# Another order of score pairs, products with V and projection visits in the first attention block of a transformer layer

## The chip, the core and the metric

The kernel runs on one core of a Trainium2 chip. The metric is the device time of one execution in microseconds (us), as the median of several runs. The engines are named as in the profile: PE is TensorE (its weight loads are PEld), DVE is VectorE, ACT is ScalarE, POOL is GpSimd and SP is SyncE, which issues most of the transfers.

## What is computed

One pre-norm transformer layer on x of 2048 rows and 512 columns, in float32, without weights in the norms:

```python
h  = x + A(layernorm(x))       # 32 heads of 16, one shared K and V
h2 = h + B(layernorm(h))

# A: q = (x @ wq) per head, k = x @ wk, v = x @ wv
#    o = softmax(q k^T / 4) v ; o @ wo
# B: (gelu(x @ w_gate) * (x @ w_up)) @ w_down,  F = 1792
```

## The kernel before

**Blocks, lists and pairs.** The 2048 rows of queries are worked through in four blocks of 512. In a block there are eight groups of four heads, and for each group sixteen chunks of 128 keys. For each group and chunk there are two score steps. One score step ("s", `pace`, which calls `score` and `scores`, line L352) is a pair of products for two heads, of 128 keys by 512 queries each, into one tile s of two PSUM banks, and one exponential on ACT over 128 x 1024 elements (L356) into half of a tile p. There are three such tiles s in turn, so the score step n needs the exponential of step n - 3 to be done. After both steps of a chunk follows the product with V ("v", `finish(1)`, which calls `weigh`, L360) into the bank `acc`: the four heads of p, each in two passes, so that a v is eight records of the profile. When a group's sixteenth v is through, `evacuate` copies `acc` to oT (DVE, L373), stores it to DRAM (`acc_d`, SP, L374), and gets it back turned (oc, L384); then DVE inverts the sums (L389), divides and splits into o_hi and o_lo. The dense part reads these.

**The first block.** Only this block concerns us. While its scores run, the queries of the later blocks are still to be projected. This is a generator (`later_q` and `project_q`) that is advanced by a "visit" ("p"): usually six products of 128 x 512 (pq, L205) of one of the four column groups of a block, so that a column group takes two visits. At the end of the second, DVE splits the result into qh and ql, squares qh into qs, and SP stores three tiles of q_d (L234). pq and pqn share the one spare bank of PSUM. When a block's four column groups are through, the products of the norms (pqn, L243) follow. Then qn is copied (DVE, L247) and its maximum taken, GpSimd forms mm (L252 to L259), and DVE forms m (L270), which SP stores (L272). The products pqn follow in the same visit or in an "n" (`norm`), which runs them if they are due and does nothing otherwise. mm and m come with the visit after that.

**Who sets the order.** It is written out by hand: a string of moves for the head, and one that is run eight times, once for each group ("list"). PE, ACT, GpSimd, DVE and SP all work through their instructions in the order in which these moves emit them.

```python
OPENING = "ssspsspsp"
PERIOD = "ssvssvssvnssvvsssvsvssvssvvssspssvvsssvvsspsssvvsnssp"
moves = {"s": pace, "p": visit, "n": norm, "v": partial(finish, 1)}
for move in OPENING + PERIOD * (PER // KC):
    moves[move]()
```

The head has six s, so the lists begin with the steps 6, 38, 70 and so on (counted from 0). A v works on the oldest chunk that waits for it; about three wait at any time. The visits end before the eighth list does.

**What hangs on the count of s.** After each fourth s, `pace` takes one step of the finished groups' output (`take_out`: the return of oc, the inversions, the division) and one step of the splitting of later weights on GpSimd (`part_weights`: loads, L125 and L126, stores w_d at L460 and L466). With the 256th s the first block's work is drained, and its memory is handed to the dense part. With the 260th s `prime` issues nine loads for the dense part on SP: three of x (xb, L519), three of w1 (L501) and three of w2 (L509). From the 279th s on, the dense part's products (pp first, L751) are woven between the scores by other, fixed strings (`CYCLES`).

Of the kernel before, what the change touches and what calls it, by code (L numbers as in the profile page):

```python
# [31 lines left out]

OPENING = "ssspsspsp"

PERIOD = "ssvssvssvnssvvsssvsvssvssvvssspssvvsssvvsspsssvvsnssp"

RUNS = ((0, 1, 2, 3), (4, 5, 6, 7), (8, 9, 10, 11), (12, 13))

# [19 lines left out]
def kernel(  # L58
# [97 lines left out]
    def run(outer, first):  # L156
# [824 lines left out]
        with tc.manual_schedule(engines={mybir.EngineType.SP, mybir.EngineType.DVE}):  # L981
# [46 lines left out]
# [3 lines that stand above are left out]
# [401 lines left out]
```

## Time and profile before

| | |
|---|---|
| median of three runs | 1429.42 us (1429.18 to 1429.70) |
| profiled execution, its own time | 1433.01 us |
| its span in the profile | 1430.9 us |
| mean granted clock of PE | 0.997 |
| PE busy | 1396.5 us (98%) |
| ACT busy | 1031.6 us (72%) |
| DVE busy | 639.4 us (45%) |
| GpSimd busy | 219.4 us (15%) |
| exponentials (L356) | 1024 of 1.04 us |
| first block's lists, start of the first to end of the eighth | 60.3 to 308.8 us |

A row of the timeline has start, length, engine, line, operation, output and inputs, shape, and the number of merged instructions; in brackets stand the idle time before it and what ended that. A row of the windows has the stretch, its length, the busy time of PE, PEld, DVE, ACT and POOL with their counts, the granted clock, the DMA engines' share and GB/s.

### The profile page before, as it was taken

What the parts mean: (1) busy time and instruction counts of PE and PEld (TensorE: products, weight loads), DVE (VectorE), ACT (ScalarE), POOL (GpSimd) and SP (SyncE); (2) the same over time, 40 slices, a digit from 0 to 9 for tenths busy, and PEclk for the clock granted to TensorE, in tenths of its full rate; (3) what the DMA queues carried; (4) which work ended last, traced back from release to release, by engine and by line L of the source; (5) the groups of instructions that cost most, each with busy time, mean ns of one, the idle gap of its engine ahead of it and who ended that gap; (6) DMA issues with size and microseconds to landing.
All of it is one profiled execution on the core that took longest, in us unless ns stands there. A gap on an engine that the chain in (4) does not pass through costs nothing.

```text
span 1430.9 us, 25109 instructions
## 1 busy us (share of the span) xinstructions
PE 1396.5 (98%) x10384; PEld 752.4 (53%) x10384; DVE 639.4 (45%) x1043; ACT 1031.6 (72%) x1147; POOL 219.4 (15%) x305
## 2 busy tenths in 40 slices
PE   6999999999999999999999999999999999999998
PEld 5433333335455555545555555545555555556876
DVE  7413131224364444455364444545354453436665
ACT  7699999997877777877777777777777777752000
POOL 5587767710000000000000000000000000001000
PEclk9999999999999999999999999999999999999999
DMA  4467667634222332312422333311332333244352
GB/s 157 140 204 237 222 216 222 226 103 177 71 90 89 111 116 101 108 64 63 168 82 78 131 101 107 108 49 42 147 101 86 115 112 104 89 148 175 126 185 76
DMA packets 66930, 180.57 MB, mean 126 GB/s; under 512 B 9436, under 2 KB 9436, under 8 KB 66776
## 3 DMA queue, kind: packets, MB, share of 16 engines
q1 hardware_dynamic: 56976, 144.79, 30.4%
q0 software_dynamic: 9760, 34.08, 7.1%
q8 instruction: 84, 1.38, 0.4%
q14 instruction: 38, 0.31, 0.1%
q10 hardware_dynamic: 72, 0.00, 0.0%
HBM read 131.13 MB, written 47.71 MB: 125 GB/s over the span
## 4 chain that ended last, share of the span: by engine, by line
PE 89%; DVE 4%; ACT 3%; DMA 1%; issue 1%; SPq 0%; ACTq 0%; DVEq 0%
PE acc L360 31%; PE s L352 19%; PE pg L751 8%; PE pd L751 8%; PE pu L751 7%; PE pq L205 4%; ACT p L356 3%; PE pd L781 3%; PE pp L751 2%; PE pu L781 2%; PE pg L781 2%; DMA w<-w_d 1%; PE pk L1219 1%; PE pd_rest L793 1%; DVE ga L644 0%
## 5 line engine op out<-in xcount | busy, mean ns | idle before, releaser
L356 ACT ACTIVATE p<-s 128x1024 f32<-128x1024 f32 x1024 | 960.8, 1039 | 241.2 <-PE s L352 240.9
L360 PE MATMUL acc<-p,v_sb 128*32 128x512 f32 x4096 | 492.6, 601 | 0.0
L352 PE MATMUL s<-qg,kaug 50*128 50x512 f32 x1984 | 389.8, 427 | 4.1 <-ACT p L356 3.6
L352 PEld LDWEIGHTS s<-qg,kaug 50*128 50x128 f32 x1984 | 171.6, 184 | 286.8 <-issue 133.0
L360 PEld LDWEIGHTS acc<-p,v_sb 128*32 128x32 f32 x4096 | 110.1, 109 | 231.7 <-issue 217.3
L751 PE MATMUL pg<-x2h,w 64*128 64x512 f32 x672 | 177.1, 394 | 4.2 <-DVE g L625 3.1
L751 PE MATMUL pu<-x2h,w 64*128 64x512 f32 x672 | 175.6, 393 | 0.0
L135 POOL TENSOR_SCALAR rstd<-mv 128x1 f32<-128x1 f32 x16 | 3.5, 220 | 977.9 <-DVE mv L133 977.8
L751 PE MATMUL pd<-w,gh 64*128 64x512 f32 x624 | 124.1, 392 | 1.4 <-DVE h L681 1.4
L681 DVE TENSOR_TENSOR h<-h,pd 128x512 f32<-128x512 f32 x80 | 54.4, 686 | 149.4 <-PE pd L751 149.4
L751 PEld LDWEIGHTS pg<-x2h,w 64*128 64x128 f32 x672 | 95.8, 185 | 20.3 <-DVE g L625 6.5
L751 PEld LDWEIGHTS pu<-x2h,w 64*128 64x128 f32 x672 | 94.7, 185 | 11.4
L751 PE MATMUL pg<-x2l,w 64*128 64x512 f32 x336 | 100.3, 391 | 0.0
L751 PE MATMUL pu<-x2l,w 64*128 64x512 f32 x336 | 99.2, 391 | 0.0
L751 PEld LDWEIGHTS pd<-w,gh 64*128 64x128 f32 x624 | 68.4, 185 | 13.1 <-DVE h L681 2.7
L890 ACT ACTIVATE ga<-ga 128x512 f32<-128x512 f32 x14 | 8.8, 632 | 92.0 <-DVE ga L887 92.0
L389 DVE RECIPROCAL oc<-oc 128x128 f32<-128x128 f32 x64 | 56.6, 922 | 34.2 <-DMA oc<-acc_d 33.8
L751 PE MATMUL pd<-w,gl 64*128 64x512 f32 x312 | 71.8, 391 | 0.0
L625 DVE TENSOR_TENSOR g<-g,pg 128x512 f32<-128x512 f32 x42 | 28.7, 684 | 91.0 <-PE pg L751 91.0
L625 DVE TENSOR_TENSOR u<-u,pu 128x512 f32<-128x512 f32 x42 | 28.9, 687 | 78.7 <-PE pu L751 78.5
L621 DVE COPY g<-pg 128x512 f32<-128x512 f32 x42 | 29.0, 691 | 74.7 <-PE pg L751 74.7
L125 DVE CAST qh<-pq 128x512 fp32r<-128x512 f32 x11 | 7.6, 689 | 114.4 <-PE pq L205 114.4
(242 smaller groups left out, 1477.7 us busy)
## 6 DMA issues: line engine op xcount, KB each, us to landing
w<-w_d SPq DMA_DIRECT2D x112, 512.0 KB
w<-w_d SPq DMA_DIRECT2D x28, 1024.0 KB
qg<-q_d SPq DMA_DIRECT2D x62, 200.0 KB
q_d<-qh SPq DMA_DIRECT2D x32, 256.0 KB
acc_d<-oT SPq DMA_DIRECT2D x32, 256.0 KB
oc<-acc_d SPq DMA_DIRECT2D x128, 64.0 KB
w_d<-w_0b POOLq DMA_DIRECT2D x14, 512.0 KB, 3.8
w_d<-w_1b POOLq DMA_DIRECT2D x14, 512.0 KB, 5.6
```

Of the source, the lines that this page charges most:

```text
L205: nc.tensor.matmul(pq, wt[:, d, c * P : (c + 1) * P], xt[:, d, :], start=(n == 0), stop=(n == 3 * DC - 1),)
L352: nc.tensor.matmul(s[:, a, :], kaug[rows, kc * P : (kc + 1) * P], qg[rows, u, :], start=True, stop=True,)
L356: nc.scalar.activation(p[:, 2 * u : 2 * u + 2, :], s, AF.Exp, scale=SCALE)
L360: nc.tensor.matmul(acc[32 * j : 32 * j + 32, :], v_sb[:, kc, :], p[:, j, :], start=(kc == 0), stop=(kc == KC - 1), skip_group_check=True,)
L389: nc.vector.reciprocal(oc[:, 1, sl], oc[:, 1, sl])
L621: nc.vector.tensor_copy(half, bank)
L625: nc.vector.tensor_tensor(half, half, bank, op=ALU.add)
L681: nc.vector.tensor_tensor(hs[b, t], hs[b, t], bank, op=ALU.add)
L751: nc.tensor.matmul(bank, lhsT[r], rhs[r], start=(k == 0), stop=(k == n - 1), skip_group_check=True,)
L781: nc.tensor.matmul(bank, lhsT, rhs, start=(i == 0), stop=(i == len(ts) - 1))
L793: nc.tensor.matmul(bank, lhsT, rhs, start=(i == 0), stop=(i == len(ts) - 1))
L1219: nc.tensor.matmul(pks[b], wt[:, c, :], xt[:, c, :], start=(c == 0 and n == 0), stop=(c == DC - 1 and n == 2),)
```

## The change

One string is another. It has the same 32 s, 16 v and three p; it has three n instead of two.

```diff
-PERIOD = "ssvssvssvnssvvsssvsvssvssvvssspssvvsssvvsspsssvvsnssp"
+PERIOD = "psssvvssvnsspsssvvssvnssvssvssvvssspssvssvvnsssvvssvss"
```

Cut at the runs of s, the two lists read:

```
before  ss v ss v ss v n ss vv sss v s v ss v ss vv sss p ss vv sss vv ss p sss vv s n ss p
after   p sss vv ss v n ss p sss vv ss v n ss v ss v ss vv sss p ss v ss vv n sss vv ss v ss
```

In the orders that the two programs emit this moves more than the products. The first visit after the head (with mm and m of the first block) stands ahead of step 6 instead of behind step 24. The products pqn of the blocks 1, 2 and 3 stand ahead of the steps 63, 146 and 235 instead of 76, 164 and 256, and their mm and m ahead of the steps 70, 155 and 237 instead of 89, 165 and, as part of the drain, 256. After step 236 no visit has products any more: the "p" ahead of step 237 has mm and m alone, and the one ahead of step 251 only the bound's check; there five s follow one another. The last v of a group comes one s later, so `take_out` returns oc four steps later and behind the load of the next qg. For the eighth group, the last v stands behind the 260th s instead of ahead of it, and so `prime`'s nine loads stand ahead of the last store of oT and the last return of oc in SP's order. The rest of the program is the same.

## The prediction

> **What bounds the kernel now.** I read the page first, then the table of windows cut at the starts of the eight lists, then the timeline of one list on TensorE, then the waits at both ends of the block.
>
> ```profile
> PE 1396.5 (98%) x10384; PEld 752.4 (53%) x10384; DVE 639.4 (45%) x1043; ACT 1031.6 (72%) x1147; POOL 219.4 (15%) x305
> L356 ACT ACTIVATE p<-s 128x1024 f32<-128x1024 f32 x1024 | 960.8, 1039 | 241.2 <-PE s L352 240.9
> ```
>
> TensorE is busy for 98% of the span. ScalarE's exponentials are the other long engine, and over the whole kernel they wait 241 us for scores. The change touches only the first of four blocks, so that block has to be read by itself. A list starts with the score step ("s") 6, 38, 70 and so on. The columns are the window, its length, PE, PEld, DVE, ACT and POOL busy, the granted clock, the DMA share and GB/s.
>
> ```profile
> 60.34:92.67 32.33, 32.28 (x213) 11.71 (x212) 6.86 (x11) 29.48 (x32) 25.57 (x31) 0.95 0.54 177
> 92.67:123.46 30.79, 30.74 (x211) 11.57 (x210) 4.26 (x5) 29.82 (x33) 22.13 (x27) 1.00 0.76 251
> 279.25:308.76 29.51, 28.62 (x203) 9.80 (x203) 4.70 (x9) 28.75 (x32) 5.91 (x9) 1.00 0.42 133
> ```
>
> List 2 is 30.8 us long with TensorE full and ScalarE 1 us short of it. So TensorE's issue is the bound there, and ScalarE is close behind. Only the last list, which has one visit of the projections instead of three, has TensorE idle (0.9 us): there ScalarE bounds. The timeline of TensorE in list 2 gives the price of each piece:
>
> ```profile
> 92.67 0.74 PE L352 MATMUL s<-qg,kaug 50*128 50x512 f32 x4
> 93.33 1.06 PE L360 MATMUL acc<-p,v_sb 128*32 128x512 f32 x8
> ...
> 97.65 0.86 PE L352 MATMUL s<-qg,kaug 50*128 50x512 f32 x4
> 98.44 1.92 PE L360 MATMUL acc<-p,v_sb 128*32 128x512 f32 x16
> 100.29 0.97 PE L352 MATMUL s<-qg,kaug 50*128 50x512 f32 x6
> 101.19 1.06 PE L360 MATMUL acc<-p,v_sb 128*32 128x512 f32 x8
> 102.19 0.50 PE L352 MATMUL s<-qg,kaug 50*128 50x512 f32 x2
> 102.61 1.06 PE L360 MATMUL acc<-p,v_sb 128*32 128x512 f32 x8
> ...
> 108.83 0.50 PE L205 MATMUL pq<-xT_hi,wq_hi 128*128 128x512 f32 x1
> ...
> 110.42 0.72 PE L352 MATMUL s<-qg,kaug 50*128 50x512 f32 x4
> ...
> 120.68 1.29 PE L352 MATMUL s<-qg,kaug 50*128 50x512 f32 x6
> 121.90 0.50 PE L205 MATMUL pq<-xT_hi,wq_hi 128*128 128x512 f32 x1
> ```
>
> From start to start: two s 0.66 us (92.67 to 93.33), but 0.79 where they wait for a score buffer (97.65 to 98.44, the row is 0.86 long instead of 0.74); three s 0.90 (100.29 to 101.19), with such a wait 1.22 (120.68 to 121.90); a lone s 0.42; one product with V ("v") 1.00 (101.19 to 102.19); two v 1.85 (98.44 to 100.29); a visit ("p") 1.59. A list of before has eight twos, five threes, one lone s, six single v, five double v and three p. Two twos and one three of it wait. Sum: 6 x 0.66 + 2 x 0.79 + 4 x 0.90 + 1.22 + 0.42 + 6.00 + 9.25 + 4.77 = 30.8, which is what the windows show.
>
> **Lists 2 to 7.** The new list has the same six single and five double v and three p, but ten twos, four threes and no lone s: 10 x 0.66 + 4 x 0.90 + 6.00 + 9.25 + 4.77 = 30.22 without waits. Where would it wait? ScalarE's pace comes from this row:
>
> ```profile
> 314.22 13.86 ACT L356 ACTIVATE p<-s 128x1024 f32<-128x1024 f32 x15 [1.84 <-PE s L352]
> ```
>
> The last of 15 takes about 1.02, so 14 steps take 12.84: 0.917 us for one, 29.3 us for 32. "ss v" takes TensorE 1.66 us and ScalarE 1.83, so each of these loses 0.17 of the lead that the three score buffers give. Before, the stretch of "ss v" three times and then "ss" makes the first wait, and two others follow later in the list. The new list has that stretch once, and its other double v and visits are spread so that the lead is restored. I keep one wait of 0.13: 30.35, or 0.44 less for each list. Six lists give -2.6 us. The bounds are 30.22 (no wait) and 30.60 (three waits as before), so -3.5 to -1.2.
>
> **The start.** The first list, at 60.34 before, now begins with a visit, where before it had none until its 19th s. The visit carries mm and m of the first block too.
>
> ```profile
> 60.44 0.68 DVE L247 COPY qn<-pqn 32x512 f32<-32x512 f32 x1 [0.47 <-PE pqn L243]
> ```
> ```profile
> 57.76:61.18 3.42, 1.83 (x13) 0.73 (x15) 2.88 (x6) 1.46 (x3) 0.00 (x0) 1.00 0.80 242
> 61.18:64.59 3.41, 3.41 (x16) 0.70 (x12) 0.65 (x1) 2.62 (x4) 1.89 (x2) 0.50 0.53 190
> ```
>
> The visit's products need the one spare bank, which holds pqn until the copy ends at 61.12. They start there, and not at 60.34 as the list's first s did, which is 0.8 us of idle TensorE. They then fall into the 3.41 us in which the clock is granted at 0.50 (its window before had TensorE busy for 1.83 of 3.42, and will have less). So the visit takes 3.2 us and that s starts at about 64.4. One list of 30.4 later the second list starts at 94.8 instead of 92.67: +2.1 us. At the full clock it would be +0.7. The visit itself isn't lost: the last list lacks one for it.
>
> **List 8 and the clock.** All visits end earlier, and two "p" of the last list find no TensorE work. Where they stood five s follow one another. Before, the one such run lies just behind the block:
>
> ```profile
> 307.14 0.96 PE L352 MATMUL s<-qg,kaug 50*128 50x512 f32 x6
> ...
> 310.11 3.46 PE L360 MATMUL acc<-p,v_sb 128*32 128x512 f32 x16
> ```
> ```profile
> 306.94:310.35 3.41, 2.34 (x18) 1.01 (x18) 1.37 (x4) 3.27 (x4) 0.17 (x1) 1.00 0.30 96
> 310.35:313.76 3.41, 3.41 (x18) 0.70 (x12) 0.00 (x0) 2.02 (x3) 0.00 (x0) 0.50 0.00 0
> ```
>
> It takes 2.97 us (307.14 to 310.11), because ScalarE must empty the buffers. List 8 sums to two such runs (5.94), seven twos (4.62), two threes (1.80), 6.00 and 9.25 for the products with V, and an estimated 1.8 for the norm's product (as a v) and the last two s: 29.4, no less than ScalarE's 29.3, and about the 29.51 of before. So the block ends at 2.1 - 2.6 + 0 = -0.5 us.
>
> The windows show a second cost of such a run: after 3.41 us with TensorE busy for 2.34 the clock fell to 0.50 for the next 3.41, and ScalarE waited 1.84 us. I price one fall at 1.6. Before has one at the block's end. After has three places for one (two runs of five in list 8, one of four behind it), each only if a window happens to hold most of the run. With no fall the change stands at -2.1, with one at -0.5, with two at +1.1, with three at +2.7. One or two are likeliest, so I take the middle: **+0.3 us**.
> The Trainium skill ("TensorE: Matmul & The Clock Gate", Why this matters for your kernels) asks only for no idle gaps above about 3 us. The trace differs: the window above has TensorE idle for 1.07 us in all. By that rule no run of s would cost a clock, and the sum would be -2.1.
>
> **SyncE's queue.** The first loads of the dense part are issued at the 260th s. Before, the last product with V of the block and its output's store and return ran ahead of them; now that product is one s later, so nine loads stand in SyncE's queue ahead of the store of oT, and the return of oc behind it.
>
> ```profile
> 308.61 0.38 SPq L374 DMA_DIRECT2D acc_d<-oT  x1
> 315.11 1.92 SPq L384 DMA_DIRECT2D oc<-acc_d  x4
> 317.51 0.35 SPq L519 DMA_DIRECT2D xb<-in_A_x_dram  x1
> ```
> ```profile
> 323.50:334.50 11.00, 10.59 (x84) 4.93 (x80) 0.95 (x2) 9.26 (x10) 0.00 (x0) 1.00 1.00 386
> ```
> ```profile
> 319.19 3.39 DVE L389 RECIPROCAL oc<-oc 128x128 f32<-128x128 f32 x4 [10.63 <-DMA oc<-acc_d]
> 323.33 0.43 DVE L125 CAST o_hi<-oc 128x512 fp32r<-128x512 f32 x1
> ```
> ```profile
> 331.63 0.45 PE L751 MATMUL pp<-wo_hi,o_hi 64*128 64x512 f32 x2
> ```
> ```profile
> 62.45 0.61 POOL L125 CAST wo_hi<-wo_raw 128x512 fp32r<-128x512 f32 x1 [5.43 <-DMA wo_raw<-in_A_wo_dram]
> ```
> ```profile
> 289.05 0.63 POOL L466 DMA_DIRECT2D w_d<-w213b  x1 [0.30 <-POOL w213b L126]
> w_d<-w_1b POOLq DMA_DIRECT2D x14, 512.0 KB, 5.6
> ```
>
> The loads need the memory of the splitting of weights, so they can start once GpSimd's last store has landed: at 289.05 + 5.6 = 294.7 if GpSimd isn't later. It is later: its mm of the first block now stands ahead of its first weight load and waits for the maximum behind the copy above, so its first cast moves from 62.45 to about 70 (an estimate: 62 for the maximum behind the copy, then mm's four short steps, then the 5.43 us of waiting for the load). With all of these 7.5 us kept the loads start at 302.2, and at 304 with the last block's mm, m and bound in front. I take 300, since GpSimd waits for its loads now and then and can win some of it back. The transfers run for 18 us (317.51 to behind 334.50), then the store lands at 319.5, oc's return takes 4.1 (315.11 to 319.19), and 4.6 later o_hi is cast (319.19 to 323.76): 328.2, at most 332.2. The tenth product of the first projection is the first to read it, at 331.63 before. So the 7.9 us of cover there shrink to some 3, and the sum takes nothing for it; if GpSimd loses more, each us counts in full.
> The Trainium skill ("DMA: Bandwidth & Descriptors", Queues, rings and completion order) says that each ring consumes descriptors in order; no row above shows it. Without it the store would land 10 us earlier and this cover would stay.
>
> Other queues: m and mm of later blocks wait on VectorE for GpSimd, with the split of the next visit queued behind. There are seven s (6.4 us at ScalarE's pace) up to it, and mm is four short steps: nothing.
>
> **Rivals.** *The queue (slower, 15%).* GpSimd's delay grows to 10.5 us, by loads that collide. Then the dense loads start at 307 and o_hi comes at 335.2, 4.1 us behind the product, which stands at 331.1 with one fall of the clock: -0.5 + 4.1 = +3.6, 1433.0. It decides from a start of 303 on. For it: GpSimd waits for its loads already (5.43 us in the row). Against: the rows above account for 304 at most.
> *Three falls of the clock (slower, 13%).* Each run in a window: +2.7, 1432.1; with 0.5 of stalls between them, 1432.6. For it: the drop above. Against: 2.97 us of run must meet a 3.41 us window three times.
> *No fall at all, and a start at full clock (faster, 10%).* By the skill's rule or by the windows' phase: -2.1 - 1.4 = -3.5, 1425.9. Against it: both drops in the trace followed half-idle windows.
> That the change doesn't do what it says is no rival: the order of TensorE's instructions is fixed by the program.
>
> **The numbers.** The profiled execution has a span of 1430.9 and a time of 1433.0; the runs' median is 1429.42, so I add the change to the median: 1429.7, with 62% for the forecast (own range 1427.3 to 1431.5). Below 0.2% (2.9 us) a measurement of this kernel can hardly tell a change from none. Faster 10%: the third rival. Slower: 14 of the first rival's 15 and 10 of the second's 13, 24%. The rest, 66%, is the same. The range reaches to 1426.6 and 1433.4 and leaves out about a tenth on each side.
>
> **What would show it.** Right: lists 2 to 7 of 30.2 to 30.6 us with one wait of s for ACT each; the second list at 94 to 95.5; one or two windows of clock 0.50 between 286 and 318; the reciprocals of the last oc at about 324 without a stop of the first projection. Wrong: lists of 30.8 or more (then the waits only moved), a product of pp that waits for o_hi, or a visit that waits for its bank.

## The result, and the profile after

The changed kernel takes 1441.33 us as the median of five runs (1437.39 to 1444.65), against 1429.58 before: a ratio of 1.0080 (95% interval 1.0062 to 1.0098). Measured once more beside other runs of before it took 1436.80 (1435.01 to 1438.36), a ratio of 1.0051 (1.0037 to 1.0064). It is slower, by 7 to 12 us. I had forecast 1429.7, with a range up to 1433.4.

The profiled execution took 1443.87 us, its span is 1442.0. Two lines of its page, busy time and the chain that ended last, and the chain of before:

```profile
PE 1399.8 (97%) x10384; PEld 751.9 (52%) x10384; DVE 638.6 (44%) x1043; ACT 1031.9 (72%) x1147; POOL 218.8 (15%) x305
...
PE 71%; DMA 9%; POOL 9%; DVE 5%; issue 3%; ACT 1%; SPq 0%; POOLq 0%; DVEq 0%; ACTq 0%
```
```profile
PE 89%; DVE 4%; ACT 3%; DMA 1%; issue 1%; SPq 0%; ACTq 0%; DVEq 0%
```

The engines have as many instructions as before, and no busy time has grown by more than 3.3 us. But the chain runs over GpSimd and the DMA transfers for 18% of the span instead of 1%, so something of theirs is waited for. The windows of the lists 1, 3, 6 and 8 (columns as in the prediction), and list 6 of before, tell where:

```profile
64.00:95.78 31.78, 31.78 (x212) 11.78 (x211) 6.57 (x9) 29.57 (x32) 21.70 (x25) 0.95 0.54 175
127.11:157.57 30.46, 30.46 (x211) 11.32 (x210) 8.74 (x11) 29.87 (x33) 23.45 (x28) 1.00 0.67 220
219.26:257.64 38.38, 32.84 (x211) 11.73 (x210) 10.96 (x16) 30.10 (x33) 26.64 (x33) 0.91 0.71 225
288.12:319.31 31.19, 28.78 (x197) 8.94 (x197) 4.85 (x9) 28.71 (x32) 12.16 (x17) 0.95 0.55 165
```
```profile
217.61:248.43 30.82, 30.76 (x211) 11.58 (x210) 3.20 (x5) 29.37 (x33) 23.22 (x30) 1.00 0.71 218
```

List 3 has about the forecast length. List 6 is 8 us too long. In it TensorE is busy for 32.84 of 38.38 us, and the clock is at 0.91. The timeline at that place, with GpSimd, VectorE and TensorE together, and the same m before:

```profile
217.10 0.26 POOL L252 TENSOR_SCALAR mm<-q,k2m 32x1 f32<-32x1 f32 x1
...
218.76 0.79 DVE L270 TENSOR_SCALAR m<-qn,mm 32x512 fp32r<-32x512 f32 x1 [17.22 <-POOL mm L259]
219.48 3.37 DVE L389 RECIPROCAL oc<-oc 128x128 f32<-128x128 f32 x4
...
225.08 0.68 DVE L373 COPY oT<-acc 128x512 f32<-128x512 f32 x1
...
225.81 3.64 PE L360 MATMUL acc<-p,v_sb 128*32 128x512 f32 x16 [5.54 <-DVE oT L373]
```
```profile
218.44 0.53 DVE L270 TENSOR_SCALAR m<-qn,mm 32x512 fp32r<-32x512 f32 x1 [1.76 <-POOL mm L259]
```

VectorE stood at m of block 2 for 17.22 us, because GpSimd formed mm only then. That is no later than before (217.10 against 216.79), but the new order needs it ten steps earlier, and GpSimd was 22 us late by then. Behind m were queued the inversions, the division and the copy of oT that frees `acc`. So TensorE stood for 5.54 us, and the clock was granted at half for 6.83 us (223.95 to 230.77). The second place is behind the block:

```profile
306.96 0.26 POOL L252 TENSOR_SCALAR mm<-q,k2m 32x1 f32<-32x1 f32 x1
...
309.18 0.33 SPq L272 DMA_DIRECT2D q_d<-m  x1
309.63 0.34 SPq L1354 DMA_DIRECT2D b_d<-q2m  x1
313.35 0.35 SPq L519 DMA_DIRECT2D xb<-in_A_x_dram  x1
...
320.84 0.33 SPq L374 DMA_DIRECT2D acc_d<-oT  x1
332.98 1.75 SPq L384 DMA_DIRECT2D oc<-acc_d  x4
...
338.00 3.39 DVE L389 RECIPROCAL oc<-oc 128x128 f32<-128x128 f32 x4 [18.80 <-DMA oc<-acc_d]
...
342.14 0.43 DVE L125 CAST o_hi<-oc 128x512 fp32r<-128x512 f32 x1
...
342.72 0.50 PE L751 MATMUL pp<-wo_hi,o_hi 64*128 64x512 f32 x2 [2.00 <-DVE o_hi L125]
```

The chain reads downwards: mm of block 3, the stores of m and of the bound, the nine loads (313.35), the store of oT behind them (320.84), its return 12.1 us later (332.98), o_hi (342.14). A fall of the clock follows (343.41 to 346.83). Against the profile of before, the exponentials are 8.9 us late ahead of this place and 12.8 behind it.

GpSimd's lateness grew on the way. Its first split is 7.9 us late (the subtraction at 71.08 instead of 63.14), the 27th 22.5 (206.58 instead of 184.04), the last 17.2 (304.66 instead of 287.46). It waits longer for its own loads: 52.8 us up to 310 us instead of 37.9, summed over all kinds. One kind has most of the difference, first before and then after (us in total, times, longest):

```profile
POOL w_1b L125 <- DMA w_1r<-in_B_w_up_dram: 12.8, 9, 5.0
```
```profile
POOL w_1b L125 <- DMA w_1r<-in_B_w_up_dram: 24.9, 9, 5.2
```

### The profile page after: what moved, and what is told of

Same layout as the page of the kernel before. It is cut to its first block, busy times and chain, and to the rows that moved or that the text cites. A ratio compares the mean times of both kernels' runs of the same rounds, so it can differ in the third digit from the quotient of the medians.

```text
span 1442.0 us, 25105 instructions
## 1 busy us (share of the span) xinstructions
PE 1399.8 (97%) x10384; PEld 751.9 (52%) x10384; DVE 638.6 (44%) x1043; ACT 1031.9 (72%) x1147; POOL 218.8 (15%) x305
## 4 chain that ended last, share of the span: by engine, by line
PE 71%; DMA 9%; POOL 9%; DVE 5%; issue 3%; ACT 1%; SPq 0%; POOLq 0%; DVEq 0%; ACTq 0%
PE acc L360 23%; PE s L352 14%; PE pg L751 8%; PE pd L751 7%; PE pu L751 7%; DMA w_1r<-in_B_w_up_dram 4%; PE pd L781 3%; PE pu L781 2%; PE pg L781 2%; PE pp L751 2%; DMA acc_d<-oT 1%; POOL w_1b L126 1%; DMA w<-w_d 1%; DMA wo_raw<-in_A_wo_dram 1%; ACT p L356 1%
## 5 line engine op out<-in xcount | busy, mean ns | idle before, releaser
L373 DVE COPY oT<-acc 128x512 f32<-128x512 f32 x32 | 22.1, 690 | 112.2 <-PE acc L360 112.1
L625 DVE TENSOR_TENSOR g<-g,pg 128x512 f32<-128x512 f32 x42 | 28.8, 685 | 90.9 <-PE pg L751 90.9
```

The costliest lines, as they stand in the source:

```text
L373: nc.vector.tensor_copy(oT, acc)
L625: nc.vector.tensor_tensor(half, half, bank, op=ALU.add)
```

## The experiments

Ratios are to runs of before on the same chip.

| run | edit | median us | ratio (95%) |
|---|---|---|---|
| e1 | changed kernel, `prime` at the 264th s | 1431.96 | 1.0014 (1.0004 to 1.0024) |
| e2 | changed kernel, GpSimd's first loads ahead of mm | 1432.60 | 1.0019 (1.0008 to 1.0030) |
| e3 | changed kernel, m on GpSimd | 1438.00 | 1.0047 (1.0034 to 1.0060) |
| e4 | leading p moved to the end | 1435.88 | 1.0037 (1.0024 to 1.0050) |
| e5 | e1 and e3 together | 1431.76 | 1.0012 (1.0001 to 1.0024) |
| e6 | e4 with `prime` at the 264th s | 1427.08 | 0.9978 (0.9969 to 0.9987) |
| e7 | before, `prime` at the 258th s | 1442.10 | 1.0084 (1.0070 to 1.0098) |
| e8 | changed kernel, three raw buffers | 1432.61 | 1.0014 (1.0005 to 1.0024) |
| e9 | changed kernel, last oT and oc by GpSimd's queue | 1430.86 | 1.0006 (0.9997 to 1.0015) |
| e10 | e6 with three raw buffers | 1427.31 | 0.9979 (0.9970 to 0.9988) |
| e11 | before, `prime` at the 264th s | 1429.47 | 0.9994 (0.9985 to 1.0004) |
| e12 | changed kernel again | 1436.80 | 1.0051 (1.0037 to 1.0064) |

**e1: the loads behind the last return.**

```diff
-                if n == 2 * PER + 4:
+                if n == 2 * PER + 8:
                     prime()
```

> The changed kernel, with the nine loads of `prime` emitted at the 264th s instead of the 260th, so behind the last store of oT and the last return of oc in SyncE's order. Theory A (GpSimd is late; that stops TensorE once in list 6, where VectorE's m waits for mm, and once behind the block, where the last oc returns behind the late dense loads): the first stop stays (about 8 us), the second goes. oT is stored at about 321, oc returns by about 331, o_hi is cast at about 335 instead of 342.1, ahead of its product at about 340.5. The lateness against before, which grew from 8.9 us at the 279th exponential to 12.8 at the 284th, stays at 8.9: 1437.5. Rival B (SyncE's order is the whole loss, and the stop in list 6 is made up behind the block): about 1430. If SyncE's order costs nothing: 1441.3 as before the edit.

Its profiled execution took 1437.18, close to the 1437.5 expected, and has the first stop alone. TensorE's wait in list 6, and SyncE's queue, in its timeline:

```profile
222.19 3.64 PE L360 MATMUL acc<-p,v_sb 128*32 128x512 f32 x16 [4.64 <-DVE oT L373]
...
315.47 0.34 SPq L374 DMA_DIRECT2D acc_d<-oT  x1
317.81 1.71 SPq L384 DMA_DIRECT2D oc<-acc_d  x4
...
320.69 0.36 SPq L519 DMA_DIRECT2D xb<-in_A_x_dram  x1
```

With nothing ahead of it the store is followed by its return after 2.3 us instead of 12.1. The later loads cost the dense part nothing: the lateness stays at 5.1 us to the last exponential. The median of the runs is 5 us lower still, 1431.96 (1428.40 to 1437.18), and only one run besides the profiled one lies above 1434. So the stop in list 6 probably has its profiled size in few of them (only the profiled one has a trace); I had expected it to stay.

**e2: GpSimd's first two loads ahead of mm.**

```diff
-            raws, left = {0: steps[0][0]()}, None
+            raws, left = {i: steps[i][0]() for i in (0, 1)}, None
+            yield 0
...
-                if i + 1 < len(steps):
+                if 1 < i + 1 < len(steps):
...
+                next(parts)
```

> The changed kernel, with GpSimd's first two weight loads issued ahead of the first block's mm, as they stood before the change; nothing else moves. Theory A: GpSimd's first cast comes at about 62.5 instead of 70.4 and the 8 us stay won: mm of block 2 comes at about 209 instead of 217, just before VectorE is needed for the copy of oT, so the stop of 5.5 us and the half clock behind it in list 6 go. The dense loads start at about 305 instead of 313, o_hi comes at about 334, 1 to 2 us behind its product: 1430 to 1432. Rival C (GpSimd's lateness is made by its loads colliding with the new places of the projections, 14 of the 22 us at block 2 growing after the start): mm of block 2 comes at 214 or later, at least 4 us of the stop stay, 1437 or more.

GpSimd's first split is 0.9 us late instead of 7.9. But the 28th is 16.8 us late again, so much of rival C is right: the lateness grows by itself in this order. mm of block 2 came at 211.11, and a stop of 1.9 us was left in list 6. Behind the block TensorE waited 3.24 us:

```profile
301.22 0.25 POOL L252 TENSOR_SCALAR mm<-q,k2m 32x1 f32<-32x1 f32 x1
...
336.97 0.79 PE L752 MATMUL pp<-wo_hi,o_hi 64*128 64x512 f32 x2 [3.24 <-DVE o_hi L125]
```

The median, 1432.60, is just above the range of theory A. The profiled execution, 1439.14, is the longest of the twelve, so its stops may be larger than those of the other runs.

**e3: m of the later blocks on GpSimd.**

```diff
-            nc.vector.tensor_scalar(m, qn, mm[:, 1:2], mm[:, 2:3], op0=ALU.mult, op1=ALU.add)
+            nc.gpsimd.tensor_scalar(m, qn, mm[:, 1:2], mm[:, 2:3], op0=ALU.mult, op1=ALU.add)
...
-            nc.sync.dma_start(q_d[hs, 3 * DH, tsl].bitcast(F32), m[hs].bitcast(F32))
+            nc.gpsimd.dma_start(q_d[hs, 3 * DH, tsl].bitcast(F32), m[hs].bitcast(F32))
```

> The changed kernel, with m of the later blocks computed on GpSimd behind mm and stored from there, so that VectorE and SyncE wait for GpSimd nowhere in the lists. GpSimd gets three steps and three stores more. Theory A: the stop in list 6 goes and its half clock with it (list 6 at about 31 us instead of 38.4; the 262nd exponential 8 us earlier). But the dense loads still wait for GpSimd's last store, at 306 or a little later, so they start at 313 to 315 and o_hi is cast at 342 to 344 as in the changed kernel, while its product is now due at about 332.5: the 8 us are given back behind the block. 1440 to 1443, no gain. A rival, in which the two stops are separate costs that add: 1433.5.

List 6 is 30.52 us long and has no stop; the exponentials are 0.9 us ahead of before at the block's end. Then 9.2 us are lost at once:

```profile
337.60 0.79 PE L751 MATMUL pp<-wo_hi,o_hi 64*128 64x512 f32 x2 [6.72 <-DVE o_hi L125]
```

So the two stops don't add. When o_hi comes is set by the loads, not by TensorE, and what is won in the lists is waited for behind the block. The median lies 2 us under what I had expected, but well above the rival's 1433.5.

**e4: the leading p at the end of the string.**

```diff
-PERIOD = "psssvvssvnsspsssvvssvnssvssvssvvssspssvssvvnsssvvssvss"
+PERIOD = "sssvvssvnsspsssvvssvnssvssvssvvssspssvssvvnsssvvssvssp"
```

> The changed string with its leading p moved to its end: lists of the same pieces, in which every visit comes one place later, so that mm and m of the blocks 0 to 3 stand ahead of the steps 13, 77, 165 and 251 (before the change 25, 89, 165, 256; in the changed kernel 6, 70, 155, 237). GpSimd's first load is ahead of mm again. Theory A: GpSimd is within 3 us of its times before, there is no stop in list 6, the lists stay at 30.2 to 30.6 us, the first list has no visit at half clock, so the 262nd exponential comes about 2 us earlier than before the change, and o_hi is ready ahead of its product: 1426.5 to 1428.5, faster than both kernels. Rival C (the pieces' new order itself makes GpSimd's loads collide): GpSimd is 10 us or more late at block 2, a stop of some us in list 6 or behind the block, 1433 or more.

The expectation missed by more than 7 us. One premise was wrong: the splitting begins with the 16th s, so mm of the first block, ahead of the step 13, still stood in front of GpSimd's first load, whose split was 8.4 us late. The lists had no stop, and TensorE was 3.2 us ahead of before at the block's end. Then it lost 13.3 us:

```profile
338.63 0.80 PE L751 MATMUL pp<-wo_hi,o_hi 64*128 64x512 f32 x2 [10.02 <-DVE o_hi L125]
```

The profiled execution, 1441.63, is again the longest: the other four took 1435.04 to 1436.25, so the loss in them is probably smaller.

**e5: e1 and e3 together** (the two diffs above).

> The changed kernel with both edits: m of the later blocks on GpSimd (no wait of VectorE in the lists) and `prime` at the 264th s (store and return of the last oc ahead of the nine loads). Theory A now reads: the loss has two places, and behind the block it is the nine loads standing ahead of the store of oT in SyncE's order (the return then comes 12 us behind the store, whenever GpSimd ended). With both places mended nothing of the loss is left: the 264th exponential 0.9 us earlier than before the change as with m on GpSimd alone, and no stop behind it: 1428.5 to 1430. If GpSimd's late end itself holds up the dense part (its loads land too late for the first products): 1434 or more.

Neither stop is in its profile, but the median is 1.8 us above the expected range: with both places mended the string as it was changed is no faster than before. Its profile has two falls of the clock, at the start (61.20) and in list 8 (300.13).

**e6: e4 with `prime` at the 264th s** (the diffs of e4 and e1).

> The string with its leading p moved to the end, and `prime` at the 264th s. In the trace of that string alone TensorE was 3.24 us ahead of before at the 264th exponential, without a stop in the lists, and lost 13.3 us behind the block to the nine loads ahead of oT. Theory A: the 13.3 us go, the 3.2 us stay: 1426 to 1427.5, faster than both kernels. If the loads are on the path when they come later (x and w1 for the first dense products), 1429 or more.

As expected, and faster than both kernels, by 0.2% against before: 0.9978. Windows of the lists 2 to 7, and of the eighth:

```profile
90.76:275.55 184.79, 184.68 (x1269) 68.68 (x1268) 45.12 (x62) 179.53 (x193) 132.40 (x159) 1.00 0.68 222
275.55:305.43 29.88, 28.56 (x204) 9.61 (x203) 4.78 (x9) 28.69 (x32) 18.80 (x24) 1.00 0.61 195
```

**e7: one thing alone, on the kernel before.** `prime` ahead of the last two products with V, as the change has it for the last one; the string is that of before.

```diff
                 n += 1
+                if n == 2 * PER + 2:
+                    prime()
                 if n % 4:
...
-                if n == 2 * PER + 4:
-                    prime()
```

> The kernel before, with one thing changed: `prime` is emitted at the 258th s, so that the nine loads stand ahead of the last store of oT in SyncE's order, as the change has it; the string, GpSimd and VectorE are as before. Theory A (the order is the cost, not GpSimd's lateness): the loads start behind m of block 3 at about 308.5, the store of oT goes out at about 316 and oc returns 12 us behind it, o_hi is cast at about 336, 4.5 us behind its product at 331.6: 1434 to 1435.5. Rival (only a late GpSimd makes the order harmful): the loads run at once behind GpSimd's last store of 289, the cover of some us holds: 1430.

This order, without the new string, costs as much as the change: 1.0084. GpSimd's last store is on time here (287.38), so its lateness isn't needed. The loads wait for the stores of m and of the bound of block 3 (SyncE's last wait ahead of L519 is 1.8 us for the bound's), and in the order of before their products and mm stand behind the 256th s:

```profile
303.95 0.25 POOL L252 TENSOR_SCALAR mm<-q,k2m 32x1 f32<-32x1 f32 x1 [15.94 <-DVE q L248]
...
310.38 0.36 SPq L519 DMA_DIRECT2D xb<-in_A_x_dram  x1
...
316.86 0.45 SPq L374 DMA_DIRECT2D acc_d<-oT  x1
330.26 1.74 SPq L384 DMA_DIRECT2D oc<-acc_d  x4
...
338.63 0.80 PE L751 MATMUL pp<-wo_hi,o_hi 64*128 64x512 f32 x2 [10.02 <-DVE o_hi L125]
```

I had expected some 4.5 us, less than half of that. o_hi came 2 us later than I reckoned (338.05), TensorE stood ready 3.2 us earlier, since no fall of the clock met it before, and the stop of 10.02 us brought a half clock of its own for 10.24 us:

```profile
332.24:342.48 10.24, 3.85 (x18) 1.49 (x22) 5.20 (x7) 1.02 (x1) 0.00 (x0) 0.50 0.16 52
```

**e8: three raw buffers, loads two steps ahead.**

```diff
-                raw = pw.tile([P, D], F32, tag="w_raw", bufs=2, ...)
+                raw = pw.tile([P, D], F32, tag="w_raw", bufs=3, ...)
...
-                if i + 1 < len(steps):
-                    raws[i + 1] = steps[i + 1][0]()
+                if i + 2 < len(steps):
+                    raws[i + 2] = steps[i + 2][0]()
```

> The changed kernel with three buffers of raw weights on GpSimd's side instead of two, each load issued two steps ahead instead of one. If GpSimd's lateness of 17 to 22 us in the lists (8 of it from the start) is time in which it waits for its own loads, it falls to 8 or less: mm of block 2 at 210 or earlier instead of 217.1 and the stop in list 6 at 3 us or less. The order of SyncE's queue stays, so some 6 us remain behind the block as with the two loads issued first: 1431 to 1434. If the loads are bound by what the queues can move, GpSimd is as late as in the changed kernel: 1440 or more.

The lateness that grows in the lists is waiting for the loads: the first split is 7.9 us late as before the edit, but then GpSimd waits only 4.4 us for loads in all, and mm of block 2 came at 198.96 and that of block 3 at 284.45, the latter 22.5 us earlier than in the changed kernel. The time is in the expected range, but not for my reason. With the order of the queue unchanged, no stop is left behind the block in its profile (the shortest of the runs), because the nine loads are through when oT is copied:

```profile
291.03 0.35 SPq L519 DMA_DIRECT2D xb<-in_A_x_dram  x1
...
308.59 0.33 SPq L374 DMA_DIRECT2D acc_d<-oT  x1
310.69 1.74 SPq L384 DMA_DIRECT2D oc<-acc_d  x4
```

**e9: another queue for the last oT.**

```diff
-            nc.sync.dma_start(acc_d[:, g % 4, :], oT)
+            queue = nc.gpsimd if b == 0 and g == NG - 1 else nc.sync
+            queue.dma_start(acc_d[:, g % 4, :], oT)
...
-                    nc.sync.dma_start(oc[r0 : r0 + DH, :, :], view[j])
+                    queue.dma_start(oc[r0 : r0 + DH, :, :], view[j])
```

> The changed kernel; only the store of the block's last oT and the four returns of its oc are issued by GpSimd instead of SyncE, so they go through GpSimd's queue while the nine loads go through SyncE's as before. If the store is late because transfers of one queue are done in order (the nine loads, 5.2 MB, are in front of it), it now lands within some 3 us and oc is back some 6 us behind the copy of oT, at about 325 instead of 338: no wait for o_hi behind the block, 1431 to 1434. If it is late because the loads take all of the memory's or the engines' rate, another queue doesn't help: oc comes back at 333 or later, 1438 to 1443.

The store was issued 0.7 us ahead of the first load here, so it had nothing to pass; the return, issued 4.9 us behind it, ran beside the nine loads of SyncE's queue:

```profile
309.64 0.62 POOL L375 DMA_DIRECT2D acc_d<-oT  x1 [4.02 <-DVE oT L373]
...
310.36 0.35 SPq L520 DMA_DIRECT2D xb<-in_A_x_dram  x1
...
314.58 2.05 POOL L385 DMA_DIRECT2D oc<-acc_d  x4 [4.32 <-DMA acc_d<-oT]
...
323.86 3.39 DVE L390 RECIPROCAL oc<-oc 128x128 f32<-128x128 f32 x4 [14.52 <-DMA w<-w_d]
...
328.01 0.43 DVE L125 CAST o_hi<-oc 128x512 fp32r<-128x512 f32 x1
```
```profile
324.00:327.00 3.00, 2.59 (x22) 0.94 (x26) 3.00 (x4) 3.00 (x4) 0.00 (x0) 1.00 1.03 411
```

No product waits for o_hi, and the time is that of before (1.0006). The row names a load as what ended the wait, but the four transfers of the return landed by 323.58, just ahead of it. The DMA engines were still full with SyncE's loads from 324 to 327 (a share of 1.03), so the return didn't wait for the loads that were issued ahead of it. From the first load to o_hi it took 17.7 us, against 27.2 to 28.8 in the two profiles of the changed kernel and in e7. So the larger part of the loss is the place in one queue. Bandwidth has a part too: from its issue to the first reciprocal the return took 9.3 us beside the loads and 3.7 to 5.0 behind them, and oc was back 15 us behind the copy of oT instead of the 6 that I had expected. The Trainium skill ("DMA: Bandwidth & Descriptors", Queues, rings and completion order) says that each DMA engine takes turns between the queues it has work for. The trace agrees: the return by GpSimd's queue had landed while the loads in SyncE's were running.

**e10: e6 with three raw buffers** (the diffs of e4, e1 and e8).

> The string with its leading p last, `prime` at the 264th s, and three raw buffers on GpSimd's side. With the first two edits no stop was left in the profile, so an earlier GpSimd has nothing to win in the block: 1426.5 to 1427.5 as without it. If GpSimd's lateness still costs in the timed runs (a wait of VectorE for mm that comes and goes), 1425 to 1426.

No difference to e6: where no product waits for what GpSimd forms, its being early wins nothing.

**e11: before with `prime` at the 264th s** (the diff of e1 on the kernel before).

> The kernel before with `prime` at the 264th s and nothing else. Its last store and return stand ahead of the loads already, so theory A expects no change: 1429.5 to 1431. Then the gain of the version with the rotated string is the string's. If the later loads by themselves help (less traffic while oc returns), about 1427, and the string wins nothing.

No change (0.9994). So what e6 wins is the string's, with its p at the end. This profile has no fall of the clock at the start or behind the block, where that of before has one each.

**e12: the changed kernel once more**, without an edit.

> The changed kernel itself once more, on this chip and with a second profile. Theory: the nine loads ahead of oT cost 9 to 12 us in every execution, so 1438 to 1443; the stop in list 6 hangs on how late GpSimd happens to be and need not have the same size (5 to 9 us in the three profiles with VectorE's wait for mm), and where it is smaller, the wait for o_hi behind the block is larger by as much, since o_hi comes when the loads are through. If the two add instead, the time scatters by the size of the stop.

The median is a little under the range. The profiled execution (1435.01, the shortest of the five) has neither stop. GpSimd was 8 us earlier at block 2 (208.87 instead of 217.10) and 9 at block 3, and the loads began at 303.78:

```profile
297.71 0.26 POOL L252 TENSOR_SCALAR mm<-q,k2m 32x1 f32<-32x1 f32 x1
...
303.78 0.35 SPq L519 DMA_DIRECT2D xb<-in_A_x_dram  x1
...
312.93 0.33 SPq L374 DMA_DIRECT2D acc_d<-oT  x1
323.07 1.74 SPq L384 DMA_DIRECT2D oc<-acc_d  x4
...
330.96 0.43 DVE L125 CAST o_hi<-oc 128x512 fp32r<-128x512 f32 x1
```

So 9 to 12 us "in every execution", as I wrote, is wrong: the loss depends on mm of block 3. From it to the first load there are 6.1 to 6.6 us in all seven profiles where the loads waited for it and VectorE forms m (6.4 after, 6.1 here), from there to the return of oc 19 to 20 where its store waits for the loads, and 8 to 9 more to o_hi: 33 to 35 us in sum. The product was due at 334.2 here (331.63 of before and 2.6 of lateness), so mm of block 3 may come at about 300.

## Why the prediction was wrong, step by step

- **Lists 2 to 7: right.** Forecast -2.6 us (bounds -3.5 to -1.2), lists of 30.35. Without the stop they are 30.46 to 30.49, and 31.2 to 31.3 where the norm's products fall. Windows of all six, first before, then the second profile of the changed kernel:

```profile
92.67:279.25 186.58, 186.20 (x1269) 70.11 (x1268) 45.95 (x61) 179.36 (x193) 140.01 (x169) 1.00 0.69 225
```
```profile
95.83:280.24 184.41, 184.41 (x1269) 68.61 (x1269) 43.55 (x60) 179.41 (x193) 136.19 (x166) 1.00 0.69 224
```

That is -2.17, with TensorE full throughout.
- **The start: right in kind, a little short.** The second list was forecast at 94.8 and began at 95.78. The half clock lasted 6.83 us instead of 3.41. In e1, without a fall at that place, it began at 93.10, +0.43 against the +0.7 given for the full clock.
- **List 8 and the clock: the price right, the base not.** Two falls were priced at 1.6 each. List 8 takes 29.81 us in e3, which has none in it, and 32.78 in e12, which has two: 1.5 each. In e12 all forecast terms can be seen without the stops: 2.6 us late from step 264 on, where the case of two falls said 1.1, and the second half clock at the start makes up the difference. But these are distances to the profile of before, an execution of 1433.01, 3.4 us above the median to which the sum was added. It has a fall at the start and one behind the block; e11 and e7, with the order of before at both places, have neither, and are 2.6 and 3.2 us ahead of it at step 264. So against the median a fall counts more than the sum said. How many a usual execution of before has isn't known. e5, with two falls and no stop, ends level with the profile of before, and its median lies 1.3 us above that of before.
- **SyncE's queue, "the sum takes nothing for it": wrong, and the main step that failed.** The mechanism was right, a term was mis-sized: the start of the loads. From there to o_hi the prediction had 28.2 us, and the two profiles give 28.8 and 27.2. But the start was put at 300, at most 304, and it was 313.35 in one profile of the changed kernel and 303.78 in the other. GpSimd's delay was put at 7.5 us at most, "since GpSimd ... can win some of it back"; at the last weights it was 17.2 in the first profile, and 8.0 in the second (last store at 297.00 instead of 289.05). And I took GpSimd's last store for what the loads wait for, with m and the bound as an addition at most. e7 shows that it is the stores of m and of the bound of block 3: there GpSimd had stored its last weights at 287.38, and the loads still began at 310.38. The cover of some 3 us had to hold a spread of 10. Made without the new string this order costs 1.0084 (e7); undone in either way it leaves 1.0006 or 1.0014 (e9, e1), which is +0.9 and +1.8 us where the whole sum was +0.3. It needs late loads: e8 and e2 leave the order of the queue, bring GpSimd forward, and leave 1.0014 and 1.0019.
- **"Other queues: ... nothing": wrong.** I compared seven s (6.4 us) with the length of mm, four short steps, and not with the work that stands ahead of mm on GpSimd. m waited 17.22 us, and the copy of oT, not the next visit's split, was what TensorE missed. e3 shows that with the queue as it is this stop adds little in the end, since the wait for o_hi takes its place. How often it occurs in timed executions isn't known: e5 is e1 without it, and the ratios are nearly the same.
- **"The visit itself isn't lost": wrong in effect.** List 8 takes 29.81 us in e3 without a visit's products and 29.88 in e6 with them, so there a visit costs nothing, and one moved to the start costs its full time (the sum had it so: list 8 no shorter, the start longer). e9 and e10 show it: each has one fall, at the start, and no stop, and e10, with its p at the end of the string, is 2.6 us ahead at step 264.
- **Rivals.** The first, the queue, is what happened. Its point, a start of the loads from 303 on, is about where the two profiles divide. At 15% it was far too unlikely: my own upper bound of 304 was past that point already.

**Still open.** Which transfers hold up GpSimd's loads, and why the same kernel has mm of block 2 at 217.10 in one execution and at 208.87 in another. Why the profiled changed kernel, 13.0 us late at the last exponential, ends 11.2 late; what follows the last exponential takes 153.0 to 155.8 us in the fourteen profiles, with the same program there. Of the 4.9 us between e1 and e6, which differ by the place of one p alone, 2.6 are that place (e9 and e10 above); the rest is the stop in list 6 and the falls of the clock, not separated.

## What to carry to other kernels

An order written by hand moves the transfers with the instructions: follow the last store of a stage and what stands ahead of it in its queue, and move the bulk loads of the next stage behind its return, or give the return another queue. Where an in-order engine waits for one that works ahead by itself, compare with the backlog that stands in front of the awaited step, not with the step's length. When a cover shrinks to a few us, the forecast should also say what happens beyond it, since here two executions of one kernel lay 10 us apart at the point that decides. And before a change is added to a median, compare the profiled execution with that median.

## What the runs showed of the hardware

- A store of 256 KB was followed by its return after 10.1 to 13.7 us behind nine loads of one queue (10.1 in e12, 12.1 after, 13.4 in e7, 13.7 in e4), and after 2.1 to 2.3 us with nothing just ahead of it (e1, e5, e8, e10). Close behind the stores of m and of the bound it was 5.8 to 6.5 us (before, e6, e11), though these move 64 KB and 0.1 KB and the DMA share was 0.00 for 3.4 of those us (310.35 to 313.76, before). Why is open.
- A return of 256 KB took 9.3 us, from its issue to the first reciprocal, by another queue beside the loads (e9), and 3.7 to 5.0 us behind them (e7, e12, after).
- The clock stays at half through a stop: 10.24 us at 0.50 in e7, in which TensorE was busy for 3.85.
- The spread of the runs goes with the granted clock in most experiments. In e8 the shortest run, 1429.27, had a mean clock of 0.998, and the longest, 1434.93, had 0.994; 0.004 of 1431 us is 5.7 us. It isn't the whole of it: in e3 and e12 the shortest run had 0.994 as well. The same instructions get two falls, one or none at the start of the block: 6.83 us of half clock in both profiles of the changed kernel, 3.41 in e9, none in e1.
